# Half of the attention units: loads merged over two batches, moved to the front, behind GpSimd's copies

## The chip, the cores and the metric

The kernel runs on one core of a Trainium2 chip. The metric is the device time of one execution in microseconds (us). Before the change it is 175.22 us, the median of three runs (174.65 to 175.56).

## What is computed

The reference is a banded attention followed by a soft mixture of experts:

```python
# q, k, v: (8 batches, 8 heads, 576 positions, 64), float32
rel  = pos[:, None] - pos[None, :]
mask_plain = (rel >= 0) & (rel < 32)                      # heads 0 to 3
mask_dil   = (rel >= 0) & (rel < 128) & (rel % 4 == 0)    # heads 4 to 7
attn = softmax(where(mask, q @ k.T / 8, -1e9)) @ v
x    = attn as (4608 tokens, 512)
logits = x @ phi                                          # phi: (512, 32 slots)
d = softmax over tokens (logits);  slot_input = d.T @ x   # (32, 512)
for e in range(8):                                        # 4 slots per expert
    slot_out[e] = relu(slot_input[e] @ w1[e]) @ w2[e]     # 512x1024, 1024x512
c = softmax over slots (logits);  out = c @ slot_out      # (4608, 512) float32
```

## The kernel before

**Units.** The attention is cut into eight units, `u` = 0 to 7. A unit is two batches (`bp = u // 2`) with the four heads of one kind: plain (`ty` = 0) or dilated (`ty` = 1). `kind(u)` returns `1 - u % 2`, so even units are dilated and odd ones plain. A unit's q, k and v are loaded by `load_unit` (line 432) with DMAs issued on GpSimd's queue (POOL) that turn float32 into bfloat16 on the way. They land in one of three slots of `stg`, slot `u % 3`, in 96 partitions: 32 rows of eight token groups by four heads for each of q, k and v. A dilated unit takes three DMAs of 576 KB, in which a partition's 18,432 bytes are one run. A plain unit takes six DMAs of 288 KB, one for each batch of q, k and v; a partition then holds two runs of 9,216 bytes, of two different heads of one batch.

**Stages of a unit.** `st_T` (line 625) transposes the slot on TensorE, in four steps `j` of 18 transposes each into `ps`, and ScalarE copies each step into `TT` (line 667). `st_S` makes the scores, ScalarE their exponentials (`PT`, line 692) and VectorE the mask (line 700). `st_V` transposes v to `VN` (lines 710 and 715). `st_P` multiplies (line 739) and divides by the sums into `XB` (lines 748 and 750); `XB` is a ring of five tiles, one for a batch and a kind. `st_X` transposes `XB` to `XT` (lines 767, 779, 780). Once both kinds of a batch are there, `st_L` makes the logits (line 794), their exponentials `expT` (line 799), the slot weights `ET` (lines 825 and 829) and adds to the slot inputs (line 838), after which the batch's two `XB` tiles are free.

**GpSimd's copies.** The transposes of a plain unit need 128 columns side by side that come from the two runs of a partition. `blocked(u)` is true for every plain unit (unit 0 is excluded, but is dilated here); for these `interleave` (line 597) has GpSimd rearrange the slot in eight copies (line 608), two for each `j`: the two of `j` = 0 go to `hTT`, the other six back into the slot.

**Weights.** The first half of expert 0's w1 is loaded as float32 by SyncE (SP) at the start, with phi behind it. All other weights come through POOL's queue, 1 MB at a time into `WD`, then into slots of `stg` and into `TT` as these come free. The second weights of experts 3 and 4 are loaded in seven groups of rows, with five tiny loads (`turn`, line 848, into `mk`) between them.

**Order.** `Prog.schedule` is a planner. Operations have a cost and a due time (`key`, from the table `DUE`: pace of units, lead of each stage); among those that could start within `TOL` of the earliest, each engine takes the one that is due first. POOL and SP keep the order of the source. Each engine then runs its list in order. POOL's list is: the loads of units 0 to 2, the first weights, then again and again a unit's load once its slot has been transposed, the copies of the next plain unit and a load of weights. Behind the attention come the first and second products of the experts (`L950`, `L1025`), the products with `c` (`L1092`, `L1143`), the scaling (`L1066`, `L1067`, `L1109`) and the stores.

Of the kernel before, what the change touches and what calls it, by code (L numbers as in the profile page):

```python
# [18 lines left out]
SCALE = 1.0 / (D ** 0.5)  # L19
TOL, LINE, FETCH0 = 0.0806, 6.2, 193  # L20
DUE = {"pace": 8.24, "T": -11.42, "Tj": 4.19, "Te": 18.27, "S": -11.29, "Si": 0.41,
       "m": 22.09, "V": 3.07, "Vg": 3.25, "P": 6.98, "Pg": 3.6, "X": 19.47, "Xb": -72.44,
       "L": 4.86, "Lb": 20.25, "x": -24.07}
CT = 72
NU = 8
QB = 96
HALO = 32
# [300 lines left out]
def bass_dilated_sliding_attn__then__soft_moe_slots_kernel(  # L328
# [23 lines left out]
    VNt = [sb(f"VN{i}", [128, 6, 2, 66]) for i in range(NVN)]  # L352
    XBt = [sb(f"XB{i}", [QB, 6, 256]) for i in range(NXB)]
    XTt = [sb(f"XT{i}", [128, 2, S]) for i in range(NXT)]
# [5 lines left out]
    id0 = sb("id0", [128, 128])  # L360
    ident = sb("ident", [128, 128])
    sel = sb("sel", [128, N_SLOTS])
    fold = sb("fold", [128, N_SLOTS], F32)
# [56 lines left out]
    b_mask = [Buf(), Buf()]  # L420
    b_id0, b_id, b_sel, b_fold, b_rowm, b_phist, b_phi = [Buf() for _ in range(7)]
    b_acc, b_psA, b_csum, b_rcs, b_rtok = [Buf() for _ in range(5)]
# [6 lines left out]
    def kind(u):  # L429
        return 1 - u % 2  # L430

    def load_unit(u):
        bp, ty, s = u // 2, kind(u), u % 3

        def f(g):
            res = []
            for t, src in enumerate((q, k, v)):
                if ty:
                    rows = src[2 * bp:2 * bp + 2].rearrange(
                        "b h (p c) d -> b (h p) (c d)", c=CT)[:, 32:64]  # L440
                    res.append(g.dma_start(
                        stg[32 * t:32 * t + 32, s, :],
                        rows.rearrange("b (r x) f -> r b (x f)", x=2)))
                    continue
                for bpar in range(2):
                    rows = src[2 * bp + bpar].rearrange(
                        "h (p c) d -> (h p) (c d)", c=CT)[32 * ty:32 * ty + 32]
                    res.append(g.dma_start(  # L448
                        stg[32 * t + bpar:32 * t + 32:2, s, :].rearrange("r (x f) -> r x f", x=2),
                        rows.rearrange("(x r) f -> r x f", x=2)))  # L450
            return res
        op("pool", f, w=[b_stg[s]], cost=3.5, sem=s_u[s], nbytes=96 * 2 * 4608 * 4, ndma=3 if ty else 6)

# [55 lines left out]
    for i in range(3):  # L509
# [52 lines left out]
    for j in range(4):  # L562
        op("dve", lambda g, j=j: g.memset(rowm[32 * j:32 * j + 8, :], 1.0), w=[b_rowm], cost=0.1)
        op("dve", lambda g, j=j: g.tensor_copy(sel[32 * j:32 * j + 32, 8 * j:8 * j + 8],
                                               ident[32 * j:32 * j + 32, 32 * j:32 * j + 8]),
           r=[b_id], w=[b_sel], cost=0.1, key=1)
        op("dve", lambda g, j=j: g.tensor_copy(fold[32 * j:32 * j + 32, :],
                                               ident[32 * j:32 * j + 32, 32 * j:32 * j + 32]),
           r=[b_id], w=[b_fold], cost=0.1, key=1)
    op("dve", lambda g: g.memset(phi_pad[:], 0.0), w=[b_phi], cost=0.4, key=1)  # L570
    for hi in range(2):
# [10 lines left out]

    def blocked(u):
        return u > 0 and kind(u) == 0

# [3 lines left out]
    def il_ap(u, j, y):  # L589
        s_ = u % 3  # L590
        if j == 0:
            ap = hTT[0:96, 1152 * y:1152 * y + 1152]
        else:
            o_ = 4608 * y + 1152 * (j - 1)
            ap = stg[0:96, s_, o_:o_ + 1152]
        return ap

    def interleave(u):
        s_ = u % 3
        for j in range(4):  # L600
            b_il[u, j] = Buf()
            for y in range(2):
                def f(g, j=j, y=y):
                    c0 = 18 * j + 9 * y
                    i_ = stg[0:96, s_, :].bitcast(F32).rearrange(
                        "r (x c w) -> r c x w", x=2, c=CT)[:, c0:c0 + 9]
                    o_ = il_ap(u, j, y).bitcast(F32).rearrange("r (c x w) -> r c x w", c=9, x=2)
                    return g.tensor_copy(o_, i_)  # L608
                op("pool", f, r=[b_stg[s_]], a=[b_il[u, j]],
                   **({"w": [b_scr]} if j == 0 and y == 0 else {}), cost=0.8, port=True)  # L610

# [13 lines left out]
    def st_T(u, j):  # L625
# [5 lines left out]
        def pe(t):  # L631
            for a in range(2):
                for kk in range(9):
                    if blocked(u):
                        i_ = t.transpose(bankb2(pt, a)[:, 96 * kk:96 * kk + 96],  # L635
                                         il_ap(u, j, a)[:, 128 * kk:128 * kk + 128],
                                         ident[0:96, 0:96])
                        continue
                    if ty:
                        c = 36 * (j // 2) + 2 * (9 * a + kk) + j % 2  # L640
                        i_ = t.transpose(bankb2(pt, a)[:, 96 * kk:96 * kk + 96],  # L641
                                         two[:, c, :], ident[0:96, 0:96])
                        continue
                    c = 18 * j + 9 * a + kk
                    for hx in range(2):
                        i_ = t.transpose(
                            bankb2(pt, a)[64 * hx:64 * hx + 64, 96 * kk:96 * kk + 96],
                            src[:, hx, c, :], ident[0:96, 0:96])
            return i_
        o = op("pe", pe, r=[b_id, b_stg[s]] +  # L650
               ([b_il[u, j]] + [b_scr] * (j == 0) if blocked(u) else []), w=[pt], alloc=[pt],
               cost=0.86 if ty == 0 and not blocked(u) else 0.75,
               mode="h" if ty == 0 and not blocked(u) else "f", n=36 if ty == 0 and not blocked(u) else 18,
               key=due(u, DUE["T"] + DUE["Tj"] * j))

# [64 lines left out]
    def st_P(u, g):  # L720
        bp, ty = u // 2, kind(u)
        bpar, h01 = g // 2, g % 2
        b = 2 * bp + bpar
# [6 lines left out]
        xb = XB[b, ty]  # L730
        pts = {(6 * g + m) // 4: U[u]["p", (6 * g + m) // 4] for m in range(6)}

        def pe(t):
            for m in range(6):
                i, x = divmod(6 * g + m, 4)
                for half in range(2):
                    o_ = 384 * half + QB * x
                    bk, po_ = (half, m) if ty == 0 else (m // 3, 3 * half + m % 3)
# [5 lines left out]
        op("pe", pe, r=list(pts.values()) + [vn], w=[po], alloc=al, cost=0.46, n=12, key=k0)  # L744

        def pv():
            return pair(po)[0:QB, :, 0:390].rearrange("p x (m d) -> p x m d", d=65)
        op("dve", lambda dv: dv.reciprocal(sbt(rv)[:], pv()[:, :, :, 64]),
           r=[po], w=[rv], alloc=[rv], cost=0.15, key=k0 + 1.0)
        op("dve", lambda dv: dv.tensor_tensor(  # L750
            sbt(xb)[:].rearrange("p m (x h d) -> p h x m d", x=2, h=2)[:, h01], pv()[:, :, :, 0:64],
            sbt(rv)[:].unsqueeze(3).to_broadcast([QB, 2, 6, 64]), AluOp.mult),
           r=[po, rv], **{"w" if h01 == 0 else "a": [xb]}, cost=0.87, key=k0 + 1.2)

    def st_X(u, bpar, x):
# [88 lines left out]

    mk = sb("mk", [15, 5, 2, 4])
    turns = []
# [9 lines left out]
    def wpair(na, nb, s_, steps):  # L856
# [4 lines left out]
        for n, st in enumerate(steps):  # L861
# [11 lines left out]
            for b in bs:  # L873
                b.parts.append((0, 8, 0, 512, pb))
                b.ready.append(o)

    W_AFTER = {2: ["w10"], 3: ["w11"], 4: ["w12"], 5: ["w13"], 6: ["w14"]}
    for u in range(NU):
# [6 lines left out]
        else:  # L885
# [327 lines left out]
```

## Time and profile before

| what | value |
|---|---|
| median of three runs | 175.22 us |
| the profiled execution | 174.82 us, of which the span from first to last instruction is 173.6 us |
| mean granted TensorE clock | 0.935 |
| busy: TensorE, VectorE, ScalarE, GpSimd | 73%, 66%, 55%, 37% of the span |
| moved by DMA | 41.28 MB; read from HBM 61.93 MB, written 9.44 MB |

The page of the profile gives, in this order, busy times, the span in 40 slices (tenths of a slice busy; one slice is 4.34 us), the DMA queues, the chain of work that ended last, the costliest groups of instructions and the DMA issues. The bytes are counted on the destination's side, so loads that turn float32 into bfloat16 show half of what they read.

### The profile page before, as it was taken

How to read it: one execution, taken by the hardware profiler on the slowest of the kernel's cores; microseconds unless marked ns; L12 is line 12 of the kernel's file. 1: busy time of each engine (PE TensorE's matmuls, PEld its weight loads, DVE VectorE, ACT ScalarE, POOL GpSimd, SP SyncE). 2: the span in 40 equal slices, each digit the busy share in tenths (PEclk: the TensorE clock that was granted, in tenths of full speed). 3: DMA queues.
4: the chain of work that ended last, by engine and by line, in shares of the span. 5: the costliest groups of instructions: out<-in, count | busy, mean ns of one | idle time of the engine just before them, and what ended most of it. 6: DMA issues, size and time to landing. Idle time of an engine off the chain costs nothing.

```text
span 173.6 us, 5093 instructions
## 1 busy us (share of the span) xinstructions
PE 127.1 (73%) x2235; PEld 98.5 (57%) x2235; DVE 115.3 (66%) x261; ACT 94.9 (55%) x145; POOL 64.3 (37%) x106
## 2 busy tenths in 40 slices
PE   0004968987889799999898789898759987699000
PEld 0004848976779588788687579576545443452000
DVE  6960059578996989978979996899540110589400
ACT  2310682878878586788788578576400110589200
POOL 7950099330696205980101762935920000000000
PEclk9999985899999999999999999999995699999955
DMA  5999999999999999999999999999999999999997
GB/s 166 286 208 193 210 232 200 215 214 216 237 208 195 216 218 210 233 220 194 215 212 219 215 215 215 215 215 217 219 204 200 212 191 197 272 382 413 436 463 311
DMA packets 10357, 41.28 MB, mean 238 GB/s; under 512 B 2016, under 2 KB 5856, under 8 KB 7008
## 3 DMA queue, kind: packets, MB, share of 16 engines
q0 software_dynamic: 7952, 30.41, 87.2%
q1 hardware_dynamic: 2384, 10.55, 15.4%
q8 instruction: 17, 0.28, 0.6%
q14 instruction: 4, 0.03, 0.0%
HBM read 61.93 MB, written 9.44 MB: 411 GB/s over the span
## 4 chain that ended last, share of the span: by engine, by line
PE 35%; DVE 24%; DMA 22%; ACT 6%; POOL 4%; issue 3%
DMA TT<-in_moe_w_dram 15%; PE ps L641 8%; DMA stg<-in_v_dram 7%; PE ps L635 7%; DVE XB L750 6%; PE ps L710 5%; DVE PT L700 5%; PE ps L685 4%; DVE WD L1066 4%; PE ps L739 3%; PE ps L794 3%; POOL TT L481 3%; PE ps L767 3%; ACT PT L692 3%; ACT TT L667 2%
## 5 line engine op out<-in xcount | busy, mean ns | idle before, releaser
L692 ACT ACTIVATE PT<-ps 128x768 bf16<-128x768 f32 x48 | 37.1, 815 | 13.1 <-PE ps L685 13.0
L667 ACT ACTIVATE TT<-ps 128x864 f32<-128x864 f32 x32 | 27.7, 898 | 17.6 <-PE ps L641 11.9
L750 DVE TENSOR_TENSOR XB<-ps,RV 96x768 bf16<-96x768 f32 x32 | 30.1, 946 | 0.5
L641 PE MATMUL ps<-ident,stg 96*128 96x96 bf16 x288 | 16.5, 224 | 15.9 <-DMA stg<-in_v_dram 15.6
L715 DVE COPY VN<-ps 128x768 bf16<-128x768 bf16 x32 | 17.1, 541 | 13.8 <-PE ps L710 13.5
L641 PEld LDWEIGHTS ps<-ident,stg 96*128 96x128 bf16 x288 | 15.3, 109 | 16.6 <-DMA stg<-in_v_dram 15.6
L739 PE MATMUL ps<-VN,PT 128*128 128x65 bf16 x384 | 17.8, 197 | 3.1 <-issue 1.4
L685 PE MATMUL ps<-TT 64*128 64x96 bf16 x384 | 15.8, 206 | 5.7 <-ACT PT L692 2.3
L710 PE MATMUL ps<-ident,TT 128*128 128x128 bf16 x192 | 16.8, 229 | 1.3 <-issue 0.6
L608 POOL COPY stg<-stg 96x576 f32<-96x576 f32 x24 | 16.8, 698 | 1.5
L739 PEld LDWEIGHTS ps<-VN,PT 128*128 128x128 bf16 x384 | 14.9, 100 | 4.1 <-issue 2.2
L685 PEld LDWEIGHTS ps<-TT 64*128 64x128 bf16 x384 | 9.7, 95 | 10.2 <-ACT PT L692 3.9
L700 DVE TENSOR_TENSOR PT<-PT,mask_d 128x768 bf16<-128x768 bf16 x24 | 15.4, 674 | 0.0
L1067 ACT ACTIVATE WD<-ps,rtok 128x256 f32<-128x256 f32 (+1 forms) x20 | 9.4, 600 | 10.2 <-PE ps L1092 10.2
L448 POOL DMA_DIRECT2D stg<-in_q_dram x8 | 4.1, 518 | 28.4 <-PE ps L641 28.4
L710 PEld LDWEIGHTS ps<-ident,TT 128*128 128x128 bf16 x192 | 11.7, 102 | 4.8 <-issue 1.3
L767 PE MATMUL ps<-ident,XB 96*128 96x96 bf16 x192 | 11.2, 207 | 1.9 <-DVE XB L750 1.6
L700 DVE TENSOR_TENSOR PT<-PT,mask_p 128x768 bf16<-128x768 bf16 x24 | 12.4, 543 | 0.1
L767 PEld LDWEIGHTS ps<-ident,XB 96*128 96x128 bf16 x192 | 9.0, 98 | 3.2 <-DVE XB L750 2.8
L780 ACT ACTIVATE XT<-ps 128x576 bf16<-128x576 bf16 x16 | 9.9, 651 | 1.8 <-PE ps L767 1.7
L635 PE MATMUL ps<-ident,stg 96*128 96x96 bf16 x216 | 10.7, 209 | 0.0
L635 PEld LDWEIGHTS ps<-ident,stg 96*128 96x128 bf16 x216 | 10.0, 99 | 0.5 <-ACT PT L692 0.2
(96 smaller groups left out, 206.5 us busy)
## 6 DMA issues: line engine op xcount, KB each, us to landing
WD<-in_moe_w_dram POOLq DMA_DIRECT2D x4, 1024.0 KB, 23.1
stg<-in_moe_w_dram POOLq DMA_DIRECT2D x3, 1024.0 KB, 29.1
out_dram<-WD SPq DMA_DIRECT2D x1, 3072.0 KB, 11.0
stg<-in_q_dram POOLq DMA_DIRECT2D x4, 576.0 KB, 17.0
stg<-in_k_dram POOLq DMA_DIRECT2D x4, 576.0 KB, 19.1
stg<-in_v_dram POOLq DMA_DIRECT2D x4, 576.0 KB, 21.5
stg<-in_q_dram POOLq DMA_DIRECT2D x8, 288.0 KB, 16.3
stg<-in_k_dram POOLq DMA_DIRECT2D x8, 288.0 KB, 18.0
```

Of the source, the lines that this page charges most:

```text
L608: return g.tensor_copy(o_, i_)
L635: i_ = t.transpose(bankb2(pt, a)[:, 96 * kk:96 * kk + 96], il_ap(u, j, a)[:, 128 * kk:128 * kk + 128], ident[0:96, 0:96])
L641: i_ = t.transpose(bankb2(pt, a)[:, 96 * kk:96 * kk + 96], two[:, c, :], ident[0:96, 0:96])
L667: return ac.activation(d, sv, ACTF.Copy)
L685: i_ = t.matmul(pair(sc)[:, hx, QB * x:QB * x + QB], win(u, 1, h01, blk_, bpar)[64 * hx:64 * hx + 64], win(u, 0, h01, blk_, bpar)[64 * hx: ...
L692: op("act", lambda ac: ac.activation(sbt(pt)[:, 0:768].rearrange("p (x n) -> p x n", x=2), pair(sc)[:, :, 0:384], ACTF.Exp, scale=SCALE), ...
L700: return dv.tensor_tensor(p_, p_, m.unsqueeze(1).to_broadcast([128, 2, 384]), AluOp.mult)
L710: i_ = t.transpose(bankb(pv)[:, 128 * m:128 * m + 128], win(u, 2, h01, m, bpar), ident[:, :])
L715: op("dve", lambda dv: dv.tensor_copy(sbt(vn)[:, :, :, 0:64], bankb(pv)[:, 0:768].rearrange("p (m x d) -> p m x d", m=6, x=2)), r=[pv], w= ...
L739: i_ = t.matmul(pair(po)[:, bk, 65 * po_:65 * po_ + 65], sbt(pts[i])[:, o_:o_ + 128], sbt(vn)[:, m, half, 0:65], start=True, stop=True)
L750: op("dve", lambda dv: dv.tensor_tensor(sbt(xb)[:].rearrange("p m (x h d) -> p h x m d", x=2, h=2)[:, h01], pv()[:, :, :, 0:64], sbt(rv)[: ...
L767: i_ = t.transpose(bankb(px)[:, QB * m:QB * m + QB], sbt(xb)[:, m, 128 * x:128 * x + 128], ident[0:QB, 0:QB])
```

## The change

- `kind(u)` becomes `u % 2`: plain units are the even ones and come first; the last unit is dilated.
- A plain unit is loaded with three DMAs, one each for q, k and v, over both batches. Rows go to partitions `t`, `t + 3`, `t + 6`, ... (`t` = 0, 1, 2 for q, k, v), and a partition's two runs are now the same head of the two batches.
- All four plain units, unit 0 among them, pass through GpSimd's copies (`J0 = (0, 0)`); `interleave(0)` stands behind the load of unit 2.
- The transposes of plain units use a permutation matrix `perm` (made once by VectorE from `ident`) in place of `ident`, which puts the rows back in order.
- The two halves of a product in `st_P` are now two batches; so a plain unit writes the `XB` tiles of both batches at once (`XBa`, one tensor for all five tiles) and takes both tiles at its first group.
- phi is loaded in runs of 256 bytes, not 128. Row order changes with it, so `st_X` transposes every second column of `XB`.
- The last tiny load among the second weights (`7` in the list of steps) is gone.
- The planner's `TOL` and `DUE` have other values.

```diff
-TOL, LINE, FETCH0 = 0.0806, 6.2, 193
-DUE = {"pace": 8.24, "T": -11.42, "Tj": 4.19, "Te": 18.27, "S": -11.29, ...}
+TOL, LINE, FETCH0 = 0.1176, 6.2, 193
+DUE = {"pace": 7.91, "T": -8.23, "Tj": 4.2, "Te": 0.05, "S": -27.93, ...}
+J0 = (0, 0)
...
     def kind(u):
-        return 1 - u % 2
+        return u % 2
...
+                rows = src[2 * bp:2 * bp + 2].rearrange("b h (p c) d -> b (h p) (c d)", c=CT)
                 if ty:
                     res.append(g.dma_start(
                         stg[32 * t:32 * t + 32, s, :],
-                        rows.rearrange("b (r x) f -> r b (x f)", x=2)))
-                    continue
-                for bpar in range(2):
-                    rows = src[2 * bp + bpar].rearrange(
-                        "h (p c) d -> (h p) (c d)", c=CT)[32 * ty:32 * ty + 32]
+                        rows[:, 32:64].rearrange("b (r x) f -> r b (x f)", x=2)))
+                else:
                     res.append(g.dma_start(
-                        stg[32 * t + bpar:32 * t + 32:2, s, :].rearrange("r (x f) -> r x f", x=2),
-                        rows.rearrange("(x r) f -> r x f", x=2)))
+                        stg[t:96:3, s, :].rearrange("r (b f) -> r b f", b=2),
+                        rows[:, 0:32].rearrange("b r f -> r b f")))
...
-    op("sp", lambda e: [e.dma_start(phi_st[:], moe_phi.rearrange("(c p) s -> p c s", p=128))],
+    op("sp", lambda e: [e.dma_start(
+        phi_st[:].rearrange("p (t x) s -> p t (x s)", x=2),
+        moe_phi.rearrange("(t p x) s -> p t (x s)", p=128, x=2))],
...
+    op("dve", lambda g: g.tensor_copy(
+        perm[:].rearrange("p (t r x) -> p t r x", t=3, x=2),
+        ident[0:96, 0:96].rearrange("p (x r t) -> p t r x", t=3, x=2)),
...
-    def blocked(u):
-        return u > 0 and kind(u) == 0
+    def blocked(u, j=3):
+        return kind(u) == 0 and j >= J0[u > 0]
...
-        if h01 == 0:
-            XB[b, ty] = tile(pXB)
-            al.append(XB[b, ty])
+        if first:
+            for b in bs:
+                XB[b, ty] = tile(pXB)
+                al.append(XB[b, ty])
...
-                                 sbt(xb)[:, m, 128 * x:128 * x + 128], ident[0:QB, 0:QB])
+                                 sbt(xb)[:, m, x::2], ident[0:QB, 0:QB])
...
+    interleave(0)
     W_AFTER = {2: ["w10"], 3: ["w11"], 4: ["w12"], 5: ["w13"], 6: ["w14"]}
...
-                    (113, 128, 8), 7, (5, 128, 8), (3, 128, 4)))
+                    (113, 128, 8), (5, 128, 8), (3, 128, 4)))
```

More of the change, by code (lines that the diff above doesn't have):

```diff
@@ L19 @@
 SCALE = 1.0 / (D ** 0.5)
[L20 to L23 removed]
+TOL, LINE, FETCH0 = 0.1176, 6.2, 193
+DUE = {"pace": 7.91, "T": -8.23, "Tj": 4.2, "Te": 0.05, "S": -27.93, "Si": 5.43,
+       "m": 55.49, "V": 0.06, "Vg": 7.06, "P": 4.3, "Pg": 4.85, "X": 8.79,
+       "Xb": -84.05, "L": 2.64, "Lb": 19.01, "x": -32.69}
 CT = 72
 NU = 8
+J0 = (0, 0)
 QB = 96
@@ L352, in bass_dilated_sliding_attn__then__soft_moe_slots_kernel @@
     VNt = [sb(f"VN{i}", [128, 6, 2, 66]) for i in range(NVN)]
-    XBt = [sb(f"XB{i}", [QB, 6, 256]) for i in range(NXB)]
+    XBa = sb("XB", [QB, NXB, 6, 256])
+    XBt = [XBa[:, i] for i in range(NXB)]
     XTt = [sb(f"XT{i}", [128, 2, S]) for i in range(NXT)]
@@ L361, in bass_dilated_sliding_attn__then__soft_moe_slots_kernel @@
     ident = sb("ident", [128, 128])
+    perm = sb("perm", [96, 96])
     sel = sb("sel", [128, N_SLOTS])
@@ L420, in bass_dilated_sliding_attn__then__soft_moe_slots_kernel @@
     b_mask = [Buf(), Buf()]
-    b_id0, b_id, b_sel, b_fold, b_rowm, b_phist, b_phi = [Buf() for _ in range(7)]
+    b_id0, b_id, b_perm, b_sel, b_fold, b_rowm, b_phist, b_phi = [Buf() for _ in range(8)]
     b_acc, b_psA, b_csum, b_rcs, b_rtok = [Buf() for _ in range(5)]
@@ L569, in bass_dilated_sliding_attn__then__soft_moe_slots_kernel @@
            r=[b_id], w=[b_fold], cost=0.1, key=1)
+    op("dve", lambda g: g.tensor_copy(
+        perm[:].rearrange("p (t r x) -> p t r x", t=3, x=2),
+        ident[0:96, 0:96].rearrange("p (x r t) -> p t r x", t=3, x=2)),
+       r=[b_id], w=[b_perm], cost=0.2, key=1)
     op("dve", lambda g: g.memset(phi_pad[:], 0.0), w=[b_phi], cost=0.4, key=1)
@@ L590, in il_ap @@
         s_ = u % 3
-        if j == 0:
+        if j == J0[u > 0]:
             ap = hTT[0:96, 1152 * y:1152 * y + 1152]
@@ L599, in interleave @@
         s_ = u % 3
-        for j in range(4):
+        for j in range(J0[u > 0], 4):
             b_il[u, j] = Buf()
@@ L609, in interleave @@
                 op("pool", f, r=[b_stg[s_]], a=[b_il[u, j]],
-                   **({"w": [b_scr]} if j == 0 and y == 0 else {}), cost=0.8, port=True)
+                   **({"w": [b_scr]} if j == J0[u > 0] and y == 0 else {}), cost=0.8, port=True)
     U = [dict() for _ in range(NU)]
@@ L633, in pe @@
                 for kk in range(9):
[L634 to L638, printed above, removed]
                     if ty:
                         c = 36 * (j // 2) + 2 * (9 * a + kk) + j % 2
-                        i_ = t.transpose(bankb2(pt, a)[:, 96 * kk:96 * kk + 96],
-                                         two[:, c, :], ident[0:96, 0:96])
-                        continue
[L644 to L648, printed above, removed]
-            return i_
[L650 to L653, printed above, removed]
+                        in_, id_ = two[:, c, :], ident[0:96, 0:96]
+                    elif blocked(u, j):
+                        in_, id_ = il_ap(u, j, a)[:, 128 * kk:128 * kk + 128], perm[:]
+                    else:
+                        for hx in range(2):
+                            i_ = t.transpose(
+                                bankb2(pt, a)[64 * hx:64 * hx + 64, 96 * kk:96 * kk + 96],
+                                src[:, hx, 18 * j + 9 * a + kk, :], perm[:])
+                        continue
+                    i_ = t.transpose(bankb2(pt, a)[:, 96 * kk:96 * kk + 96], in_, id_)
+            return i_
+        o = op("pe", pe, r=[b_id if ty else b_perm, b_stg[s]] +
+               ([b_il[u, j]] + [b_scr] * (j == J0[u > 0]) if blocked(u, j) else []), w=[pt], alloc=[pt],
+               cost=0.86 if ty == 0 and not blocked(u, j) else 0.75,
+               mode="h" if ty == 0 and not blocked(u, j) else "f", n=36 if ty == 0 and not blocked(u, j) else 18,
                key=due(u, DUE["T"] + DUE["Tj"] * j))
@@ L722, in st_P @@
         bpar, h01 = g // 2, g % 2
-        b = 2 * bp + bpar
+        bs = [2 * bp + bpar] if ty else [2 * bp, 2 * bp + 1]
+        first = h01 == 0 if ty else g == 0
         po, rv = tile(psum, 2), tile(pRV)
@@ L726, in st_P, with xi @@
         al = [po]
-        if h01 == 0:
-            XB[b, ty] = tile(pXB)
-            al.append(XB[b, ty])
-        xb = XB[b, ty]
+        if first:
+            for b in bs:
+                XB[b, ty] = tile(pXB)
+                al.append(XB[b, ty])
+        xbs = [XB[b, ty] for b in bs]
+        def xi():
+            return [xb.phys[0] for xb in xbs]
         pts = {(6 * g + m) // 4: U[u]["p", (6 * g + m) // 4] for m in range(6)}
@@ L737, in pe @@
                     o_ = 384 * half + QB * x
-                    bk, po_ = (half, m) if ty == 0 else (m // 3, 3 * half + m % 3)
+                    bk, po_ = (half ^ (xi()[0] > xi()[1]), m) if ty == 0 else (m // 3, 3 * half + m % 3)
                     i_ = t.matmul(pair(po)[:, bk, 65 * po_:65 * po_ + 65],
@@ L743, in st_P @@
         k0 = due(u, DUE["P"] + DUE["Pg"] * g)
-        op("pe", pe, r=list(pts.values()) + [vn], w=[po], alloc=al, cost=0.46, n=12, key=k0)
+        o = op("pe", pe, r=list(pts.values()) + [vn], w=[po], alloc=al, cost=0.46, n=12, key=k0,
+               after=[] if first else U[u]["o", bs[0]])
+        U[u].setdefault(("o", bs[0]), []).append(o)
         def pv():
@@ L749, in st_P, with dst @@
            r=[po], w=[rv], alloc=[rv], cost=0.15, key=k0 + 1.0)
+        def dst():
+            if ty:
+                return sbt(xbs[0]).rearrange("p m (x h d) -> p h x m d", x=2, h=2)[:, h01]
+            lo, hi = sorted(xi())
+            c = 128 * bpar + 64 * h01
+            return XBa[:, lo:hi + 1:hi - lo, :, c:c + 64]
         op("dve", lambda dv: dv.tensor_tensor(
-            sbt(xb)[:].rearrange("p m (x h d) -> p h x m d", x=2, h=2)[:, h01], pv()[:, :, :, 0:64],
+            dst(), pv()[:, :, :, 0:64],
             sbt(rv)[:].unsqueeze(3).to_broadcast([QB, 2, 6, 64]), AluOp.mult),
-           r=[po, rv], **{"w" if h01 == 0 else "a": [xb]}, cost=0.87, key=k0 + 1.2)
+           r=[po, rv], **{"w" if first else "a": xbs}, cost=0.87, key=k0 + 1.2)
     def st_X(u, bpar, x):
```

6 lines of the change are left out of this document (2 added, 4 removed).

## The prediction

> **What bounds the kernel now.** I read the slices of the span first, then the stretches of time with their DMA share, then the end of the chain of waits, then the DMA issues.
>
> ```profile
> DMA  5999999999999999999999999999999999999997
> GB/s 166 286 208 193 210 232 200 215 214 216 237 208 195 216 218 210 233 220 194 215 212 219 215 215 215 215 215 217 219 204 200 212 191 197 272 382 413 436 463 311
> PE 35%; DVE 24%; DMA 22%; ACT 6%; POOL 4%; issue 3%
> 24.00:129.00 105.00, 92.18 (x1893) 77.69 (x1892) 89.72 (x187) 73.93 (x107) 52.49 (x81) 0.97 1.02 214
> 96.00:127.00 31.00, 26.32 (x531) 21.09 (x524) 26.61 (x60) 19.28 (x31) 20.36 (x29) 1.00 1.03 216
> 149.00:151.00 2.00, 1.15 (x12) 0.60 (x10) 1.21 (x3) 1.33 (x4) 0.00 (x0) 1.00 1.07 257
> 151.00:173.00 22.00, 8.62 (x40) 3.78 (x40) 10.45 (x17) 9.23 (x18) 0.00 (x0) 0.81 1.00 413
> ...
> 119.00 0.57 POOL TT L481
> ...
> 125.93 25.25 DMA TT<-in_moe_w_dram
> ...
> 151.22 0.32 PE ps L1025 x4
> ...
> 158.56 3.95 DVE WD L1066 x6
> ```
>
> The DMA engines are full (9) in every slice but the first and last; in the stretch rows the last two columns are DMA share and GB/s: 1.02 and 214 through the attention, 1.00 and 413 in the stores. In the attention TensorE is busy 92.18 of 105 us and VectorE 89.72, so both have idle time; the DMA engines have none. The chain by engines misleads: its 35% of TensorE lie before 119 us, where the last weights are issued, and those then wait 25.25 us, mostly behind other loads:
>
> ```profile
> stg<-in_v_dram POOLq DMA_DIRECT2D x8, 288.0 KB, 19.9
> TT<-in_moe_w_dram POOLq DMA_DIRECT2D x1, 1024.0 KB, 21.2
> ```
>
> At 216 GB/s 1 MB takes 4.9 us; it lands 21.2 us after its issue, so some 16 us of loads stood ahead of it. The time is therefore first gap + bytes / rate. A change that moves no bytes can only gain by making their transport cheaper, and can lose only by letting the queue run dry.
>
> **Three DMAs for six.** Two stretches carry only a plain or only a dilated unit, of equal length and bytes:
>
> ```profile
> DMA packets 190, 1.18 MB, mean 214 GB/s; under 512 B 63, under 2 KB 63, under 8 KB 63
> ...
> q0 software_dynamic: 189, 1.16, 102.2%
> DMA packets 96, 1.18 MB, mean 214 GB/s; under 512 B 32, under 2 KB 32, under 8 KB 32
> ...
> q0 software_dynamic: 95, 1.16, 99.6%
> L448 POOL DMA_DIRECT2D stg<-in_q_dram x8 | 4.1, 518 | 28.4 <-PE ps L641 28.4
> ```
>
> The first pair of rows (61.0 to 66.5 us) is plain, the second (74.0 to 79.5 us) dilated. Plain costs 102.2% against 99.6% of 16 engines for 5.5 us: 2.6% x 5.5 x 16 = 2.3 us of engine time for 94 more packets, 31 small (completions) and 63 large. That is 24 ns each. Three DMAs fewer a unit are 3 x 16 = 48 small packets; four units 192; 192 x 24 ns / 16 engines = 0.30 us less. Bounds: nothing, as both rows say 214 GB/s; or all of the 2.6%, 2.3 us x (1.73 / 1.16 MB) x 4 / 16 = 0.86 us, if the partition's two runs became one packet too. The source still has two runs, so I take 0.30. On POOL 12 issues of 518 ns go, 6.2 us that nothing waits for.
>
> [...]
>
> **phi and the tiny load.**
>
> ```profile
> q1 hardware_dynamic: 543, 0.12, 47.0%
> DMA packets 521, 0.98 MB, mean 197 GB/s; under 512 B 401, under 2 KB 401, under 8 KB 401
> ```
>
> The first row is 5.0 to 6.2 us: 0.56 us of all engines, of which about 0.13 us is the end of the weights ahead (0.055 MB at the stores' 413 GB/s), so phi's 512 packets cost 0.43 us. Half as many of twice the size save between nothing and 0.21; I take 0.10. The second row is 128 to 133 us, where the five tiny loads run: 197 for 216 GB/s is 0.44 us lost in 5 us; the one removed is 7 of 32 tiny rows, 0.10 us (nothing to 0.2).
>
> **Unit 0 behind copies.**
>
> ```profile
> 15.56 5.86 PE ps L641 x72
> 10.33 0.59 POOL L481 DMA_DIRECT2D WD<-in_moe_w_dram  x1
> 21.70 1.03 POOL L448 DMA_DIRECT2D stg<-in_q_dram  x2 [10.79 <-PE ps L641]
> 24.68 1.87 POOL L608 COPY hTT<-stg 96x576 f32<-96x576 f32 x2
> 26.61 4.71 POOL L608 COPY stg<-stg 96x576 f32<-96x576 f32 x6
> 96.36 1.77 POOL L608 COPY hTT<-stg 96x576 f32<-96x576 f32 x2 [3.64 <-DMA stg<-in_v_dram]
> 98.19 4.50 POOL L608 COPY stg<-stg 96x576 f32<-96x576 f32 x6
> 105.62 1.53 PE ps L635 x36
> ```
>
> Now the transposes start at landing, 15.56, and end 5.86 later, at 21.42. After, POOL waits for that landing, copies for 1.87 + 4.71 = 6.6 us, and the last quarter of the transposes (1.5) follows: 23.7, so 2.2 us later. Behind the new wait on POOL stand the first weights (issued at 10.33 now, about 22 then) and the load of unit 3 (21.70 now, about 24 then). Cover: units 0 to 2 are 5.3 MB, 25 us at 214 GB/s from about 5.5 us, so the engines are fed until 30. Price 0; without the cover, the lateness beyond 8 us.
>
> At the other end the copies leave the last unit: now they wait for its landing until 96.36, end at 102.7, and its transposes at 107.15. After, the last unit, dilated, needs only the landing. I credit nothing for it but expect it to repay the 2.2 us before the last unit ends.
>
> **No effect on the path.**
>
> ```profile
> L710 PEld LDWEIGHTS ps<-ident,TT 128*128 128x128 bf16 x192 | 11.7, 102 | 4.8 <-issue 1.3 <-DVE XB L750 1.3 <-DVE VN L715 0.9
> L641 PEld LDWEIGHTS ps<-ident,stg 96*128 96x128 bf16 x288 | 15.3, 109 | 16.6 <-DMA stg<-in_v_dram 15.6 <-ACT TT L667 0.3 <-issue 0.3
> L750 DVE TENSOR_TENSOR XB<-ps,RV 96x768 bf16<-96x768 f32 x32 | 30.1, 946 | 0.5
> ```
>
> Reading every second column of `XB`: L710 reads `TT` so at 102 ns, L641 reads side by side at 109, so nothing. The division keeps its 768 elements and its 946 ns. `perm` is one copy while VectorE waits for the first landing.
>
> The new order matters only if work behind the attention turns late. Its cover there:
>
> ```profile
> 142.05 1.69 PE L1161 MATMUL ps<-wrm 128*128 128x512 bf16 x7
> 145.50 0.60 PE L1161 MATMUL ps<-wrm 128*128 128x512 bf16 x2
> 146.82 0.10 PEld L1025 LDWEIGHTS ps<-TT,hTT 128*32 128x32 bf16 x4 [0.69 <-DMA TT<-in_moe_w_dram]
> 148.65 2.58 SPq L1058 DMA_DIRECT2D out_dram<-WD  x4
> ```
>
> TensorE fills 1.69 + 0.60 us with idle products and waits 0.69 for weights before the first half's stores at 148.65: 3.0 us of cover. The stores must be there when the loads run out between 149 and 151; each us later than that is a us of idle engines.
>
> **Sum.** 0.30 + 0.10 + 0.10 = 0.50 us less. The profiled execution took 174.82 (span 173.6 and 1.2 around it), so 174.3 for its like; it lies 0.40 below the median, so against 175.22 I forecast 174.7. One measurement tells about 0.5% (0.9 us) from no change; this is 0.3%.
>
> **Rivals.**
>
> *The attention ends late (slower).* A plain unit now claims two of the five `XB` tiles at its first group, and a batch's tiles come free only behind its logits:
>
> ```profile
> 122.13 0.65 ACT L799 ACTIVATE expT<-ps 128x576 bf16<-128x576 f32 x1 [1.31 <-PE ps L794]
> 125.32 0.51 PE L838 MATMUL ps<-XB,ET 96*32 96x256 bf16 x12
> ```
>
> From exponential to slot inputs that is 3.7 us. Should the last plain unit wait once for such a chain and the start's 2.2 us not be repaid, the second products are 5.9 us late, 2.9 beyond the cover: 174.7 + 2.9 = 177.6. It decides from 3.0 us of lateness. For: in the order built from the changed code the first product (L739's) of units 2, 4 and 6 each stands some four rows behind the slot inputs of the batch that frees its tiles, where the old order had it ahead of them. Against: there is other work of TensorE between the two; VectorE has 15 us of idle time in 105; the last unit is freed of copies. Chance 0.20.
>
> *Transport gains its upper bound (faster).* One packet for two runs (0.86), phi 0.21, tiny load 0.2, all three at once: 1.3 us, 173.9. For: the 2.6% are measured. Against: equal GB/s, two runs in the source. A gain beyond the rates could only come from the change-over at 149 to 151 us, 257 GB/s between 216 and 413. Chance 0.22.
>
> *It does not do what it says.* Small packets cost nothing and the engines' data rate alone counts: only phi and the tiny load stay, 0.2 us, 175.0. [...] Chance 0.06.
>
> **Numbers.** Forecast 0.52, own range 174.2 to 175.2 (sum's bounds near their middle, and the runs' spread of 0.45 either way). Faster by over 0.5%, below 174.34: the upper-bound rival 0.22 and the forecast's low end 0.08, 0.30. Slower, above 176.10: the late attention, 0.20. Same: 0.44 + 0.06 = 0.50. The range leaves out the farther half of the late attention and little below the upper-bound gain: 173.7 to 176.8.
>
> **What would show it.** Right: DMA share of 9 in all inner slices; small packets in a plain stretch halved, its share between 99.6% and 102.2%; unit 0's transposes ending near 23.7 with the slices after it still full; last weights landing about 0.5 us before 151.2. Wrong: a slice with DMA below 9 between 20 and 150 us; TensorE waiting for VectorE or `XB` rather than for weights after 142 us; the first stores issued later than 148.65 while the last weights land earlier.

## The result, and the profile after

| kernel | median us | runs | lowest to highest us |
|---|---|---|---|
| before | 174.65 | 22 | 174.25 to 175.83 |
| after | 174.10 | 22 | 173.73 to 174.79 |

The ratio of after to before is 0.9964, with a 95% interval from 0.9953 to 0.9975: 0.44 to 0.82 us less. The profiled execution took 174.04 us (span 172.8), against 174.82 before. The forecast was 174.7, no change by the bound of 0.5%. Times and ratios here and below leave out slow executions, over 1.5% above the fastest of the same kernel.

The slices of the kernel after, then its stretches (the last two columns are DMA share and GB/s), show the same bound. The DMA engines are full in every inner slice. What differs is the change-over at 149 to 151 us: 383 GB/s, where it was 257, as the loads run out 0.8 us earlier in it.

```profile
DMA  5999999999999999999999999999999999999997
GB/s 171 262 216 226 207 211 211 242 205 200 219 215 212 248 204 193 220 217 214 240 211 198 216 212 214 214 218 218 218 207 211 210 193 197 294 369 425 431 453 313
```

```profile
24.00:129.00 105.00, 93.80 (x1914) 77.92 (x1913) 88.96 (x188) 74.95 (x109) 41.11 (x64) 1.00 1.03 215
96.00:127.00 31.00, 26.77 (x524) 21.51 (x524) 25.67 (x59) 18.42 (x30) 13.88 (x20) 1.00 1.03 216
149.00:151.00 2.00, 0.58 (x8) 0.20 (x8) 0.34 (x2) 0.20 (x1) 0.00 (x0) 1.00 1.10 383
151.00:173.00 22.00, 8.22 (x35) 3.68 (x36) 10.20 (x17) 9.24 (x18) 0.00 (x0) 0.77 0.95 394
```

The end of the chain in time order (start, us, engine):

```profile
115.01 0.57 POOL TT L480
...
121.94 28.41 DMA TT<-in_moe_w_dram
...
150.39 0.32 PE ps L1042 x4
...
157.73 3.95 DVE WD L1083 x6
```

The last weights land at 121.94 + 28.41 = 150.35 us; before it was 125.93 + 25.25 = 151.18. They are issued 4.0 us earlier (115.01 for 119.00) and land only 0.83 us earlier, because they wait in a full queue. What follows them takes as long as before, so the 0.83 us is the whole gain of 0.8 us in the span.

The time hangs on the loads in the experiments below too. Take the end of the last packet of POOL's queue as the end of the loads (150.83 us before, 150.02 after). In nine of the profiled executions, before and after among them, the time is 23.98 to 24.02 us more than that. Two others (experiments 5 and 9) have 24.2, and the three whose first stores come late (experiments 1, 2 and the second of 6) have 28.4, 29.4 and 25.5.

Two rows of SyncE's queue mark this in every kernel below: the first half's stores (x4), and the first store behind the last weights (x1, 0.41 us). The first fence is before, the second after.

```profile
148.65 2.58 SPq L1058 DMA_DIRECT2D out_dram<-WD  x4
153.05 0.41 SPq L1057 DMA_DIRECT2D out_dram<-WD  x1
```

```profile
147.52 2.58 SPq L1075 DMA_DIRECT2D out_dram<-WD  x4
152.22 0.41 SPq L1074 DMA_DIRECT2D out_dram<-WD  x1
```

**The start.** GpSimd's and TensorE's timelines of the kernel after, unit 0:

```profile
14.49 1.38 POOL L613 COPY hTT<-stg 96x576 f32<-96x576 f32 x2 [5.48 <-DMA stg<-in_v_dram]
15.94 4.29 POOL L613 COPY stg<-stg 96x576 f32<-96x576 f32 x6
20.18 0.55 POOL L480 DMA_DIRECT2D WD<-in_moe_w_dram  x1
22.20 0.51 POOL L443 DMA_DIRECT2D stg<-in_q_dram  x1 [1.47 <-PE ps L650]
```

```profile
15.93 1.62 PE L650 MATMUL ps<-perm,hTT 96*128 96x96 bf16 x18 [15.93 <-POOL hTT L613]
17.38 4.52 PE L650 MATMUL ps<-perm,stg 96*128 96x96 bf16 x54
```

Unit 0 lands at 14.49, and its transposes end at 17.38 + 4.52 = 21.90: they follow the copies step by step rather than all behind them. The load of unit 3 is issued at 22.20 (21.70 before).

**The end of the attention.** The slot inputs' copy `siT`, the first work behind the attention, in the timelines of before and after:

```profile
131.70 0.28 ACT L936 ACTIVATE siT<-ps 128x32 bf16<-128x32 f32 x2 [5.54 <-PE ps L928]
```

```profile
129.72 0.28 ACT L953 ACTIVATE siT<-ps 128x32 bf16<-128x32 f32 x2 [5.24 <-PE ps L945]
```

It is 2.0 us earlier. TensorE's waits between it and the first stores have grown with that; filler products and waits for weights of the kernel after:

```profile
138.53 1.25 PE L1178 MATMUL ps<-wrm 128*128 128x512 bf16 x5
141.02 0.39 PE L1042 MATMUL ps<-stg,hTT 128*32 128x512 bf16 x1 [1.24 <-DMA TT<-in_moe_w_dram]
143.78 0.60 PE L1178 MATMUL ps<-wrm 128*128 128x512 bf16 x2
144.36 0.10 PEld L1042 LDWEIGHTS ps<-TT,hTT 128*32 128x32 bf16 x4 [0.47 <-DMA TT<-in_moe_w_dram]
145.69 0.29 PE L1042 MATMUL ps<-TT,hTT 128*32 128x256 bf16 x4 [1.04 <-DMA TT<-in_moe_w_dram]
```

From the first filler to the next weights (138.53 to 141.02), from the second to its weights (143.78 to 144.36) and the last wait (1.04) it is 4.1 us in which TensorE only waits for weights. That is the cover: lateness up to 4.1 us costs nothing.

### The profile page after: what moved, and what is told of

Its sections match the earlier page's. It is cut to its first block, busy times and chain, and to the rows that moved or that the text cites. A ratio compares the mean times of both kernels' runs of the same rounds, so it can differ in the third digit from the quotient of the medians.

```text
span 172.8 us, 5073 instructions
## 1 busy us (share of the span) xinstructions
PE 126.0 (73%) x2232; PEld 96.9 (56%) x2233; DVE 112.3 (65%) x261; ACT 95.3 (55%) x146; POOL 56.3 (33%) x93
## 4 chain that ended last, share of the span: by engine, by line
DMA 50%; DVE 18%; PE 15%; POOL 6%; ACT 3%; issue 1%
DMA stg<-in_v_dram 33%; DMA TT<-in_moe_w_dram 16%; PE ps L650 8%; DVE XB L766 4%; DVE WD L1083 4%; POOL TT L480 3%; DVE VN L717 2%; DVE PT L702 2%; DVE stg L1083 2%; ACT TT L669 2%; PE ps L712 1%; PE ps L783 1%; POOL hTT L928 1%; POOL stg L443 1%; PE ps L810 1%
## 5 line engine op out<-in xcount | busy, mean ns | idle before, releaser
L694 ACT ACTIVATE PT<-ps 128x768 bf16<-128x768 f32 x48 | 36.5, 814 | 8.8 <-PE ps L687 8.7
L669 ACT ACTIVATE TT<-ps 128x864 f32<-128x864 f32 x32 | 28.4, 902 | 20.6 <-PE ps L650 20.3
L650 PE MATMUL ps<-ident,stg 96*128 96x96 bf16 x288 | 14.7, 206 | 2.2 <-DMA stg<-in_v_dram 1.9
L650 PE MATMUL ps<-perm,hTT 96*128 96x96 bf16 x72 | 4.4, 225 | 15.9 <-POOL hTT L613 15.9
L650 PEld LDWEIGHTS ps<-ident,stg 96*128 96x128 bf16 x288 | 12.9, 98 | 3.1 <-DVE PT L702 2.1
L702 DVE TENSOR_TENSOR PT<-PT,mask_d 128x768 bf16<-128x768 bf16 x24 | 13.2, 581 | 0.0
L650 PEld LDWEIGHTS ps<-perm,hTT 96*128 96x128 bf16 x72 | 3.8, 108 | 16.1 <-POOL hTT L613 15.9
L650 PE MATMUL ps<-perm,stg 96*128 96x96 bf16 x216 | 12.6, 224 | 0.2 <-ACT TT L669 0.2
L796 ACT ACTIVATE XT<-ps 128x576 bf16<-128x576 bf16 x17 | 10.7, 654 | 2.4 <-PE ps L783 2.4
L650 PEld LDWEIGHTS ps<-perm,stg 96*128 96x128 bf16 x216 | 11.5, 108 | 0.5 <-ACT TT L669 0.3
```

The costliest lines, as they stand in the source:

```text
L650: i_ = t.transpose(bankb2(pt, a)[:, 96 * kk:96 * kk + 96], in_, id_)
L669: return ac.activation(d, sv, ACTF.Copy)
L694: op("act", lambda ac: ac.activation(sbt(pt)[:, 0:768].rearrange("p (x n) -> p x n", x=2), pair(sc)[:, :, 0:384], ACTF.Exp, scale=SCALE), ...
L702: return dv.tensor_tensor(p_, p_, m.unsqueeze(1).to_broadcast([128, 2, 384]), AluOp.mult)
L796: return en.activation(d, s_, ACTF.Copy)
```

## The experiments

The theory is that of the prediction: transport alone. By it a load costs less where there are fewer small packets, longer runs and no tiny load, and everything else hides behind the full queue. The rivals: the new order gains something of its own (because the old attention ended late, or otherwise), and removed DMAs cost nothing. Each ratio is to the kernel before, run beside that experiment; times from different groups of runs are less comparable, as the kernel before has medians from 174.6 to 175.2 us in them.

For each load I also worked out the time it occupies the queue: the packets of POOL's queue added up in order of time and cut at each load's known bytes. These "stage times" are worked out from the traces' packets. "Loads end" is the last such packet: 150.83 us before; 150.02, 149.95 and 150.08 in three traces of the kernel after. The packets' durations added up and divided by 16 engines are the "packet time" of the queue: 151.37 us before; 150.64, 150.65 and 150.63 in those three.

**1. More DMAs for the same bytes.** From the kernel after:

```diff
-   res.append(g.dma_start(stg[t:96:3, s, :].rearrange("r (b f) -> r b f", b=2), rows[:, 0:32]...))
+   for b in range(2):
+       for y in range(2):
+           res.append(g.dma_start(stg[t + 48 * y:min(t + 48 * y + 48, 96):3, s, 4608 * b:4608 * b + 4608],
+                                  rows[b, 16 * y:16 * y + 16]))
    # dilated units: one DMA for each of the two batches
```

> The changed kernel with every load of a unit cut into more DMAs of the same runs: six for a dilated unit, twelve for a plain one, 48 DMAs more in all, no byte and no large packet more. Theory (transport: each DMA costs its 16 small packets, 24 ns each): 48 x 16 x 24 ns / 16 engines = 1.15 us more, 175.25 us. Rival (completions are free; the gain came from the order or the planner): no change, 174.1 us.

Measured: 179.02 us, ratio 1.0217 (1.0174 to 1.0260). Two things are in it. The queue: loads end at 150.93, 0.91 us later for 48 DMAs, which is 19 ns for each DMA. And the rest:

```profile
DMA  5999999998999999999999999999999999299998
GB/s 180 252 211 211 219 201 207 230 236 186 214 211 210 251 203 189 214 213 214 235 202 209 210 219 217 212 221 215 213 206 219 189 197 137 91 390 409 466 412 353
```

One slice shows DMA at 2.

```profile
138.99 0.29 ACT L956 ACTIVATE siT<-ps 128x32 bf16<-128x32 f32 x2 [5.57 <-PE ps L948]
153.44 2.57 SPq L1078 DMA_DIRECT2D out_dram<-WD  x4
```

`siT` comes at 138.99, 9.3 us later than after, and the first stores at 153.44, so the engines run empty behind the loads. Lateness less cover is 9.3 - 4.1 = 5.2 us; the stores are 5.9 later. What made the attention late (48 more issues ahead of the copies on POOL is the obvious candidate) was not isolated.

**2. The new transport in the old order.** From the kernel after:

```diff
-TOL, DUE = 0.1176, {new}
+TOL, DUE = 0.0806, {as before}
-        return u % 2
+        return 1 - u % 2
```

> The changed kernel with the order of before: dilated units first, unit 0 without copies, the planner's old numbers. It keeps the three transport edits (three DMAs for a plain unit, phi in 256 bytes, no last tiny load). Theory (transport): the whole gain stays, 174.1 us. Rival (order and planner made the gain): 174.65 us, as before.

Measured: 178.86 us, ratio 1.0224 (1.0175 to 1.0274). Neither number came: this is the rival "the attention ends late".

```profile
DMA  5999998999999999999999999999999997299998
```

```profile
140.12 0.29 ACT L954 ACTIVATE siT<-ps 128x32 bf16<-128x32 f32 x2 [6.14 <-PE ps L946]
154.02 2.58 SPq L1076 DMA_DIRECT2D out_dram<-WD  x4
```

VectorE's wait before the division, in the kernel before and here (total, times, longest):

```profile
DVE RV L748 <- PE ps L739: 2.8, 5, 0.7
```

```profile
DVE RV L757 <- PE ps L746: 10.6, 9, 2.7
```

`siT` is 140.12 - 131.70 = 8.4 us later than before. Less the prediction's cover of 3.0 us that leaves 5.4; the first stores are issued at 154.02, 5.4 us later than 148.65. VectorE waits 10.6 us for the products that the division reads, where it waited 2.8 before. Loads end at 150.48, 0.35 us earlier than before, but one trace does not show that this is the transport's (experiment 5 has 150.22 with the old transport); whatever it gained was lost on the empty engines. Of the rival its place and price are shown; that the `XB` tiles cause it is not.

**3. The new order with the old transport.** From the kernel after: six DMAs for a plain unit, phi in runs of 128 bytes, the tiny load `7` back. It was run twice.

```diff
-   res.append(g.dma_start(stg[t:96:3, s, :]...  # both batches
+   for b in range(2):
+       res.append(g.dma_start(stg[t:96:3, s, 4608 * b:4608 * b + 4608], rows[b, 0:32]))
-   moe_phi.rearrange("(t p x) s -> p t (x s)", p=128, x=2)
+   moe_phi.rearrange("(c p) s -> p c s", p=128)
-   (113, 128, 8), (5, 128, 8), (3, 128, 4)
+   (113, 128, 8), 7, (5, 128, 8), (3, 128, 4)
```

> The complement: the changed kernel's order, copies and planner, but six DMAs for a plain unit (one for each batch), phi in 128 bytes and the last tiny load back. Theory (transport): the whole gain is gone, 174.65 us. Rival (order and planner): the gain stays, 174.1 us.

> The new order and planner constants with the old transport (six DMAs for the two plain units, phi in runs of 128 bytes, the last tiny load among the second weights). Transport theory (the gain is the bytes' overhead alone): the time of the kernel before, about 174.6 us, and the changed kernel 0.2 to 0.45 us below this one. Order theory (the new order spares something that the old one loses in most executions, not in its best): the lowest time is the old kernel's lowest, the median 0.3 to 0.4 us below the old one's, about 174.25, and the changed kernel another 0.2 us lower.

Measured: 174.22 us, ratio 0.9958 (0.9938 to 0.9979), and 174.38 us, ratio 0.9944 (0.9919 to 0.9968). The kernel before beside them took 175.02 and 175.16. The theory wanted the time of before; it falls. The order alone makes the kernel faster. ("Order" here is all that was left in: the order of the units, unit 0 behind copies, the rows' new places and the planner's values. They were not run apart.) SyncE's rows of the second trace:

```profile
148.00 2.93 SPq L1075 DMA_DIRECT2D out_dram<-WD  x4
152.53 0.41 SPq L1074 DMA_DIRECT2D out_dram<-WD  x1
```

The store behind the last weights is 0.5 us earlier than before (153.05) and 0.3 later than after (152.22). Loads end at 150.24 and 150.31, also between the two. The packet time is 150.92 and 150.93 us, 0.28 more than after.

**4. Fewer DMAs still.** From the kernel after, the second weights of experts 3 and 4 in one DMA, without the four tiny loads:

```diff
-   (0, 128, 2), 15, (1, 49, 8), 2, (49, 65, 8), 6, (65, 113, 8), 2, (113, 128, 8), (5, 128, 8), (3, 128, 4)
+   (0, 128, 1),
```

> The changed kernel with the second weights of experts 3 and 4 in one DMA of 2 MB: no tiny load and no group of rows left. Theory (tiny loads only cost): the remaining loss of the stretch goes, about 0.25 us less, 173.85 us. [...]

Measured: 174.79 us, ratio 0.9985 (0.9960 to 1.0009): 0.7 us slower than after, and 0.6 slower than the order alone, which ran beside it.

```profile
152.86 0.41 SPq L1073 DMA_DIRECT2D out_dram<-WD  x1
```

The stage of these weights is 0.23 us shorter (9.78 for 10.01) and the last one, experts 6 and 7, 0.9 us longer (12.48 for 11.59). The packet time is 150.31 us, 0.33 less than after, yet loads end at 150.70, 0.68 later: there is less work and it is spread less evenly. The last 16 packets of more than 4 bytes end over 0.58 us, where it was 0.35. So the groups of rows and the tiny loads between them do not only cost: with both, the queue's last packets end closer together and 0.68 us earlier. Which of the two does it was not run apart, and how is not shown, as no trace here names the engine of a packet.

**5. The old kernel with an earlier attention.** From the kernel before, the masks of units 6 and 7 cover 8 positions only; the rest of those two units' mask is left out.

```diff
+            if u >= 6:
+                return dv.tensor_tensor(p_[:, :, 0:8], p_[:, :, 0:8], m[:, 0:8]..., AluOp.mult)
```

> The kernel before, its order unchanged, with the masks of units 6 and 7 applied to 8 of 384 columns only (that part of the masking is left out): 12 of VectorE's 0.55 us become short, so the attention ends up to 5 us earlier while every DMA stays as it is. Theory T2 (in some executions of before the attention ends too late and the first stores come late; cover 2.6 us): the median falls by about 0.4 us to near its lowest runs, ratio 0.997 to 0.998, and the spread shrinks below 1 us. Theory T1 (transport alone): no change, ratio 1.000, spread as before.

Measured: 174.77 us, ratio 1.0013 (0.9989 to 1.0037).

```profile
129.06 0.28 ACT L938 ACTIVATE siT<-ps 128x32 bf16<-128x32 f32 x2 [5.51 <-PE ps L930]
```

`siT` is 2.6 us earlier than before, even earlier than after, and nothing is gained. That the old attention ends late is not what the order mends.

**6. The new kernel with a later attention.** From the kernel after, four or eight idle writes of VectorE between the last sum and the slot inputs:

```diff
+    for _ in range(4):   # 8 in the second
+        op("dve", lambda vv: vv.memset(psA_sb[:], 0.0), r=[b_acc, t_acc], w=[b_psA], cost=0.01, key=K1)
```

> The changed kernel with four clearings of psA_sb (0.49 us each) on VectorE ahead of the copy to psA_sb: the expert products start 1.9 us later, where they start in before; every DMA as in the changed kernel. T2: the cover falls from 4.3 to 2.4 us, the median rises by 0.1 to 0.4 us and single runs over 175 us appear. T1: 174.1 us, as the changed kernel.

> The same with eight clearings: 3.9 us later, cover 0.4 us. T2: most runs are late by some of their spread, median 174.6 to 175.3 us, upper runs over 176. T1: still 174.1 us.

Measured: 174.33 us, ratio 0.9984 (0.9955 to 1.0013), and 175.39 us, ratio 1.0037 (1.0011 to 1.0062). The first, then the second:

```profile
132.89 0.29 ACT L955 ACTIVATE siT<-ps 128x32 bf16<-128x32 f32 x2 [8.20 <-PE ps L947]
147.20 2.58 SPq L1077 DMA_DIRECT2D out_dram<-WD  x4
```

```profile
135.21 0.29 ACT L955 ACTIVATE siT<-ps 128x32 bf16<-128x32 f32 x2 [10.83 <-PE ps L947]
149.22 2.58 SPq L1077 DMA_DIRECT2D out_dram<-WD  x4
```

The writes made `siT` 3.2 and 5.5 us late, where 1.9 and 3.9 were expected. 3.2 us of lateness does not move the first stores (147.20 for 147.52); 5.5 us moves them by 1.7, where 5.5 - 4.1 = 1.4. The cover is about as read from the timeline. The median is 0.3 us higher already in the first, though its traced execution lost nothing (173.69 us) and the intervals overlap; that with less cover left more executions lose something would fit, but is not shown.

**7. The kernel after again,** unchanged, beside the others:

> The changed kernel unchanged, beside the others on one chip, for its spread and a second trace. Both theories: ratio 0.9964 to the kernel before; T2 moreover: its spread is below 1 us where that of before is 1.5 us or more.

> The changed kernel, unchanged, on the same chip as the three others, so that each is compared with it directly. Both theories: 174.1 us, a ratio of 0.9955 to 0.9975 to the kernel before. Transport theory: 0.2 to 0.45 us below the kernel with the order alone and 0.2 to 0.3 us below the one with phi and the tiny load alone; order theory: 0.2 and 0.4 us.

Measured: 174.06 us, ratio 0.9973 (0.9950 to 0.9995), and 174.09 us, ratio 0.9927 (0.9898 to 0.9956). The second stood beside the second run of the order alone: 0.29 us lower (174.09 and 174.38; lowest 173.73 and 174.05), though the two intervals overlap.

**8. phi and the tiny load alone,** in the kernel before:

```diff
-   moe_phi.rearrange("(c p) s -> p c s", p=128)
+   moe_phi.rearrange("(t p x) s -> p t (x s)", p=128, x=2)
-   (113, 128, 8), 7, (5, 128, 8), (3, 128, 4)
+   (113, 128, 8), (5, 128, 8), (3, 128, 4)
```

> The kernel before with two of the transport edits alone: phi in runs of 256 bytes, and no last tiny load among the second weights. Order and planner stay. Transport theory: 0.10 + 0.10 us less than before, 174.4 us, a ratio of 0.9988 (the prediction's two smaller terms; up to 0.4 us by their bounds). Order theory: the same 0.2 us or less, since the old order stays; a ratio at 0.996 would say that the order counts for nothing.

Measured: 174.85 us, ratio 0.9973 (0.9943 to 1.0003), which by itself decides nothing.

```profile
153.09 0.41 SPq L1059 DMA_DIRECT2D out_dram<-WD  x1
```

In the trace nothing is gained: the store behind the last weights is where it was (153.05). The stage of experts 3 and 4 is 0.27 shorter, but most of that is not the tiny load. In the trace of before, the 8,192-byte packets that start from 128 to 136 us take 654 ns on average (625 in the median), which is 0.35 us of all engines; in every other kernel with these loads uncut it is 626 to 636 ns, here 626. The last stage is 0.32 longer (11.97 for 11.65), and the last 16 packets of more than 4 bytes end over 0.60 us for 0.46: again less packet time (151.13 for 151.37), less evenly spread.

**9. More DMAs away from the copies.** From the kernel after, four loads of weights in eight DMAs of 16 rows each:

```diff
-   [g.dma_start(dst, vs)]
+   [g.dma_start(dst[16 * i:16 * i + 16], vs[16 * i:16 * i + 16]) for i in range(8)]   # w11, w13, w25, w21 with w22
```

> The changed kernel with 28 more DMAs in places far from the copies: four loads of weights (w11, w13, w25 and the pair 21 and 22) each in eight DMAs of 16 rows. By the prediction's price, 16 small packets of 24 ns for each DMA spread over 16 engines, 28 x 24 ns = 0.67 us more, about 174.75 us and a ratio of 1.0039 to the changed kernel. Rival (what completes a DMA costs nothing in a full queue): the changed kernel's own time, 174.1 us.

Measured: 179.40 us, ratio 1.0202 (1.0146 to 1.0257), 4.6 us over what was expected. It doesn't measure the price of a DMA. The stretches of this kernel, then of the kernel after:

```profile
116.00:122.00 6.00, 5.04 (x113) 4.03 (x112) 6.00 (x16) 3.55 (x6) 3.57 (x8) 1.00 1.10 157
122.00:128.00 6.00, 4.61 (x70) 3.67 (x66) 3.82 (x8) 3.02 (x6) 6.00 (x8) 1.00 1.07 147
```

```profile
116.00:122.00 6.00, 4.31 (x80) 3.52 (x78) 5.20 (x11) 4.21 (x8) 6.00 (x8) 1.00 1.02 214
122.00:128.00 6.00, 4.48 (x76) 3.47 (x76) 2.45 (x9) 0.74 (x2) 0.75 (x2) 1.00 1.04 216
```

The engines are busy (1.10, 1.07) and move 157 and 147 GB/s for 214 and 216: the packets are slower, 873 and 909 ns on average for 8,192 bytes, where 625 is the median elsewhere. The load of the pair w21, w22 takes 13.40 us for 9.79, the three others 0.4 to 0.7 more each. Spread over 128 rows the same bytes go at 214 to 216 GB/s; cut in blocks of 16 neighbouring rows they don't. Why is not shown, nor why the three other loads, cut in the same way, lost only 8 to 13%.

## Why the prediction came out as it did

**What bounds the kernel: right.** DMA is 9 in all inner slices, the last weights land 0.83 us earlier, the span shrinks by 0.8, and the time is the loads' end and 24.0 us more in nine traces.

**The number: right in size, by a wrong split, so partly by luck.** The forecast of 174.7 stood on the median of three runs, 175.22; over 22 runs before is 174.65, 0.57 lower, and that is nearly the whole distance from 174.7 to 174.1. The difference forecast was 0.52, the one measured 0.55. But the transport carried only a part. In the one group with all three kernels the medians are 175.16 before, 174.38 with the order alone and 174.09 after: of 1.07 us the transport has 0.29. By the loads' end (150.83, 150.28, 150.02 on average) it has 0.26 of 0.81, so a third at most:

| term | forecast us | in the runs |
|---|---|---|
| three DMAs for six, 12 fewer | 0.30 | stage times of units 2, 4, 6: 24.93 after and 24.93, 24.92 in its repeats, 25.14 and 25.15 with six DMAs: 0.22 for 9 DMAs, 24 ns each; experiment 1: 19 ns each; so 0.23 to 0.29 |
| phi | 0.10 | its packets: 512 of 13.0 ns before, 256 of 18.0 ns after, 0.13 us less (sums of 6.66 and 4.61 us, divided by 16 engines) |
| last tiny load | 0.10 | 4-byte packets from 128 to 133 us with the new order: 0.31 and 0.32 with five tiny loads, 0.27 to 0.29 with four, so 0.04; the last stage 0.1 longer |
| all of it | 0.50 | packet time 0.28 and phi's 0.13 less, 0.41; loads end 0.26 earlier than with the order alone, the median 0.29 lower |
| new order | 0 | the order alone 0.42% (0.21 to 0.62) and 0.56% (0.32 to 0.81) below before; loads end 0.55 earlier |

*Three DMAs for six.* The 24 ns per small packet were about right: the 4-byte packets of POOL's queue, 16 to a DMA (32 for the two DMAs' worth of the dilated stretch below), take 18.8 ns on average after, and a full queue shows 19 to 24 ns of its time for each DMA. The sign named for it decides little, though. DMA packets and POOL's queue in the kernel after, first 61.0 to 66.5 us (dilated), then 74.0 to 79.5 (plain):

```profile
DMA packets 98, 1.19 MB, mean 217 GB/s; under 512 B 32, under 2 KB 32, under 8 KB 32
...
q0 software_dynamic: 95, 1.16, 100.8%
```

```profile
DMA packets 159, 1.18 MB, mean 214 GB/s; under 512 B 32, under 2 KB 32, under 8 KB 32
...
q0 software_dynamic: 158, 1.16, 101.2%
```

The small packets of the plain stretch are halved, 32 for 63, and its share of 101.2% lies where it was forecast; but the dilated one, in which nothing changed, moved from 99.6% to 100.8%. A cut of 5.5 us is too short for a per cent. Stage times were needed.

*phi and the tiny load.* phi's term was about right. The tiny load's was not, and its row was misread: of the 0.44 us lost from 128 to 133 us before, 0.34 are slow large packets of that one execution. With the order alone the same five tiny loads leave 207 and 210 GB/s there, not 197. Adding the terms also failed at the end: 0.41 us of packet time spared made the loads end only 0.26 earlier. Why no more came is not shown; in experiments 4 and 8, where packet time was spared too, the last packets ended further apart (0.58 and 0.60 us for 0.35 and 0.46).

*Unit 0 behind copies.* Price 0 was right. The working wasn't: the transposes end at 21.90, not 23.7, because the unit lands 1.07 us earlier (why is not shown) and the transposes run between the copies; the forecast put the last quarter behind all of them. The load of unit 3 moved by 0.5 us, not 2.3.

*"The new order matters only if work behind the attention turns late."* This is the sentence that was wrong. The order, priced at nothing, is faster in both runs with the old transport, and it has two thirds to three quarters of the gain (0.78 of 1.07 us by the medians, 0.55 of 0.81 by the loads' end). What it mends stays open. It is not the late attention (experiment 5), and it is not the units' loads: their eight stages add up to 66.96 us before and 66.96 and 67.17 with the order alone. In the traces the gain lies in the stages behind the units (56.36 us before, 56.38 in experiment 8, 55.96 and 55.86 with the order alone). There the trace of before loses 0.35 us on the slow packets named in experiment 8, a good part of the 0.8 us between the two profiled executions. The other traces of the old order lose 0.13 (experiment 5) or nothing (experiment 8) on them, and neither of these kernels is clearly faster than before, so these packets are not shown to be the cause. What the times show is steadiness. The middle half of the runs lies between 174.14 and 174.53 with the order alone, and between 174.75 and 175.72 for the kernel before beside it, while the lowest are 174.04 and 174.05 against 174.11 and 174.37. In all groups the kernel after has medians from 174.06 to 174.10, that of before from 174.60 to 175.16; so the order's worth depends on the group, and 0.8 us is what it had in two of them.

**The rivals.** The late attention did not come in this change, and the kernel of experiment 2 shows it with its place and price: with the changed code, the new order and its due times together are what keeps it away. The upper-bound gain did not come: both traces have 768 packets of 9,216 bytes, so two runs did not become one packet. (Its 0.86 mixes two kinds of MB; 1.77 / 1.16 gives 0.87, which changes nothing.) "Small packets cost nothing" is refuted by the stage times (0.22 us for 9 DMAs).

## What to carry to other kernels

Where the DMA engines are full from end to end, read what an edit is worth from the landing of the last load (the time was that and 24.0 us in nine traces here), and price each DMA by its small packets (here 16 of 18.8 ns, and 19 to 24 ns of the queue's time); the packet times added up over the whole queue repeat within 0.02 us here, where shares of short stretches don't tell it. Look at a slow stretch in a second trace before pricing it. Small terms at the end of a queue need not add up: in experiment 4 the packet time fell by 0.33 us and the loads ended 0.68 us later. An order that seems to matter only through lateness should be run alone, with the old transport, before it is priced at nothing.

## What had not been expected of the hardware

A load cut into blocks of 16 neighbouring rows moved 147 to 157 GB/s with full DMA engines (shares of 1.07 and 1.10), where the same bytes in DMAs over 128 rows moved 214 to 216. Removing four loads of a few rows, with the groups around them merged into one DMA, made the kernel 0.7 us slower. And lateness less the cover gave the first stores of three late kernels within 0.7 us (experiments 1, 2 and the second of 6).
